# Early loads, idle transposes, split banks and weight sums made by need, in a kernel of linear attention and four experts

## The chip, the cores and the metric

One core of a Trainium2 chip. The metric is the device time of one execution in microseconds (us).

## The reference, cut to what matters

```python
# attention: batch 8, heads 8, sequence 576, head size 64
kv  = einsum('bhsd,bhse->bhde', k, v)
o   = einsum('bhsd,bhde->bhse', q, kv)
x   = o / sqrt(mean(o*o, -1) + 1e-6) * g_norm          # -> 4608 tokens x 512
# experts: E = 4, F = 1024
p   = probs / (probs.sum(-1) + 1e-9)
out = sum over e of  p[:, e] * (relu(x @ w1[e]) @ w2[e])
```

## The kernel before

The matrix products of the experts go by a scheme of the Strassen kind: seven products take the place of eight, at two levels in the first layer (49 small products for one step) and at one in the second. The price is sums: of weights, of tokens and of results. The work runs in 36 steps (4 experts x 9 chunks of 512 tokens). The attention of the eight batches is woven into the steps of the first expert, and each of the three later experts needs its sums of weights before its first step. The change of expert is called a switch below: steps 8 to 9, 17 to 18, 26 to 27.

A planner written in the kernel fixes the issue order of every engine while the kernel is built. Each operation has a key (about the step in which it is wanted) and a cost in us for each engine that may run it; the planner gives an operation to the first engine that is free in its model. Each engine then works through its list in order.

```python
def either(n):                       # a sum of n columns: VectorE or GpSimd
    return {"DVE": 0.17 + 0.00108 * n, "POOL": 0.1 + 0.0025 * n}

def combine(key, cost, out_, a, b, op, reads, writes):      # every sum of two SBUF tiles
    plan.add(key, cost, lambda eng: adder(eng).tensor_tensor(...), reads=reads, writes=writes)

BANKS = {"ub": 4, "db": 2, "ab": 2}   # PSUM banks: up-products, down-products, attention

def weights_1(e, key, step):          # first-layer weights of expert e: 4 loads, then
    ...
    form(key + 4 * step, 5, 21, 4, ALU.add)          # 4 sums of 128x1024
    ...
    for j, m in enumerate(OUTER):                    # and 7 x 4 sums of 128x256
        k2 = key + (8 + j) * step
        ...

attention(0, -2.0, 1.3, 0.1)
weights_1(0, -0.9, 0.02)
x_views = {0: x_forms(0, -0.2, 0.02)}                # sums of tokens: 4 + 7 x 4
...
            if e + 1 < E and c == NCH - 1:
                weights_1(e + 1, s + 0.0, 0.12)      # loads from s on, sums at s + 0.48 to s + 1.68
                weights_2(e + 1, s + 1.0, 0.12)
```

`POOL` is GpSimd, `DVE` is VectorE, `ACT` is ScalarE, `PE` is TensorE. The tiles lie in SBUF; PE writes its products into the eight PSUM banks of `BANKS`.

## Time and profile before

| | us |
|---|---|
| median of 6 runs | 1820.9 (1818.4 to 1821.4) |
| PE busy | 1784.6 of a span of 1818.3 |
| first expert product | 41.8 |
| first first-layer product of step 1 / 2 / 8 | 84.4 / 151.5 / 496.2 |
| last first-layer product (step 35) | 1790.8 |

### The profile page before, as it was taken

What the parts mean: (1) busy time and instruction counts of PE and PEld (TensorE: products, weight loads), DVE (VectorE), ACT (ScalarE), POOL (GpSimd) and SP (SyncE); (2) the same over time, 40 slices, a digit from 0 to 9 for tenths busy, and PEclk for the clock granted to TensorE, in tenths of its full rate; (3) what the DMA queues carried; (4) which work ended last, traced back from release to release, by engine and by line L of the source; (5) the groups of instructions that cost most, each with busy time, mean ns of one, the idle gap of its engine ahead of it and who ended that gap; (6) DMA issues with size and microseconds to landing.
All of it is one profiled execution on the core that took longest, in us unless ns stands there. A gap on an engine that the chain in (4) does not pass through costs nothing.

```text
span 1818.3 us, 32290 instructions
## 1 busy us (share of the span) xinstructions
PE 1784.6 (98%) x12496; PEld 1660.7 (91%) x12496; DVE 1126.2 (62%) x1841; ACT 608.4 (33%) x1345; POOL 475.1 (26%) x426
## 2 busy tenths in 40 slices
PE   5899999999999999999999999999999999999999
PEld 4889999999999999999999999999999999999997
DVE  6866665666676555555666555555566655556554
ACT  2544344443333333333333333333333333333331
POOL 4565554646364000000145000000036100000001
PEclk7999999999999999999999999999999999999999
DMA  9764444424433333334434333333434333343321
GB/s 231 179 167 141 128 139 126 135 95 139 132 109 119 117 114 115 114 113 134 136 130 152 118 118 118 118 118 121 147 127 163 117 115 117 118 118 116 115 74 35
DMA packets 192089, 228.96 MB, mean 126 GB/s; under 512 B 54464, under 2 KB 123328, under 8 KB 191936
## 3 DMA queue, kind: packets, MB, share of 16 engines
q1 hardware_dynamic: 191936, 226.89, 40.9%
q8 instruction: 99, 1.62, 0.4%
q14 instruction: 54, 0.44, 0.1%
HBM read 160.18 MB, written 66.65 MB: 125 GB/s over the span
## 4 chain that ended last, share of the span: by engine, by line
PE 94%; DVE 2%; SPq 2%; DMA 1%; issue 1%; POOL 0%; ACT 0%; DVEq 0%; ACTq 0%
PE ub L697 42%; PE db L831 29%; PE ab L831 18%; SPq L282 1%; PE ab L504 1%; PE ab L486 1%; DVE big L276 1%; PE ab L514 1%; PE ab L471 1%; DVE small L276 0%; DMA big<-in_moe_w_dram 0%; DMA small<-in_q_dram 0%; PE ab L553 0%; DVE big L718 0%; POOL big L276 0%
## 5 line engine op out<-in xcount | busy, mean ns | idle before, releaser
L831 PE MATMUL db<-big,big 128*128 128x256 f32 x2520 | 596.3, 380 | 1.7 <-DVE big L276 1.3
L697 PEld LDWEIGHTS ub<-small,big 128*128 128x128 f32 x3816 | 498.4, 192 | 23.4 <-issue 1.4
L697 PE MATMUL ub<-small,big 128*128 128x128 f32 x3816 | 513.5, 276 | 0.4 <-DVE big L718 0.4
L276 DVE TENSOR_TENSOR big<-big,big 128x1024 f32<-128x1024 f32 x343 | 474.8, 1384 | 55.1 <-ACT big L680 33.2
L831 PEld LDWEIGHTS db<-big,big 128*128 128x128 f32 x2520 | 455.2, 190 | 51.7 <-DVE big L276 1.5
L276 POOL TENSOR_TENSOR big<-big,big 128x1024 f32<-128x1024 f32 x85 | 209.0, 2462 | 1116.7 <-DVE big L276 976.1
L710 ACT ACTIVATE snap<-ub 128x256 f32<-128x256 f32 x756 | 285.5, 383 | 556.7 <-PE ub L697 500.8
L718 DVE TENSOR_TENSOR big<-ub,snap 128x256 f32<-128x256 f32 x756 | 307.0, 421 | 216.7 <-PE ub L697 163.1
L697 PE MATMUL ub<-small,w1y 128*128 128x128 f32 x2916 | 384.9, 276 | 2.2 <-DVE big L718 2.1
L697 PEld LDWEIGHTS ub<-small,w1y 128*128 128x128 f32 x2916 | 360.5, 192 | 7.9 <-DVE big L718 2.9
L831 PE MATMUL ab<-big,big 128*128 128x256 f32 x1512 | 357.4, 380 | 1.7 <-DVE small L788 1.7
L831 PEld LDWEIGHTS ab<-big,big 128*128 128x128 f32 x1512 | 273.2, 190 | 32.0 <-DVE small L788 2.1
L710 ACT ACTIVATE big<-ub 128x256 f32<-128x256 f32 x252 | 96.7, 384 | 414.6 <-PE ub L697 410.1
L788 DVE SCALAR_TENSOR_TENSOR small<-db,p_all,small 128x256 f32<-128x256 f32 x243 | 116.9, 481 | 139.8 <-PE db L831 139.2
L788 DVE SCALAR_TENSOR_TENSOR small<-ab,p_all,small 128x256 f32<-128x256 f32 x189 | 91.1, 482 | 177.3 <-PE ab L831 177.3
L680 ACT ACTIVATE big<-big 128x1024 f32<-128x1024 f32 x144 | 152.0, 1055 | 107.8 <-DVE big L276 104.8
L784 DVE TENSOR_SCALAR small<-db,p_all 128x256 f32<-128x256 f32 x72 | 34.6, 481 | 54.1 <-PE db L831 54.1
L425 POOL TENSOR_TENSOR rt<-ss,mhalf 128x8 f32<-128x8 f32 (+1 forms) x40 | 65.7, 1643 | 3.3
L421 POOL TENSOR_SCALAR ss<-ss 128x8 f32<-128x8 f32 (+1 forms) x40 | 15.6, 391 | 101.0 <-DVE ss L416 99.6
L416 DVE TENSOR_REDUCE ss<-small 128x8 f32<-128x512 f32 (+1 forms) x40 | 27.1, 678 | 22.3 <-ACT small L411 22.3
L504 PE MATMUL ab<-kvbd,small 128*128 128x128 f32 x256 | 38.3, 298 | 1.6 <-ACT kvbd L494 1.6
L432 DVE TENSOR_TENSOR small<-ab,rt 128x512 f32<-128x512 f32 (+1 forms) x40 | 27.4, 686 | 17.3 <-POOL rt L425 17.1
(63 smaller groups left out, 664.0 us busy)
## 6 DMA issues: line engine op xcount, KB each, us to landing
small<-x SPq DMA_DIRECT2D x189, 256.0 KB, 3.5
small<-x SPq DMA_DIRECT2D x189, 192.0 KB, 2.9
o<-small SPq DMA_DIRECT2D x108, 256.0 KB, 2.0
small<-o SPq DMA_DIRECT2D x108, 256.0 KB, 2.8
big<-in_moe_w_dram SPq DMA_DIRECT2D x32, 512.0 KB, 5.0
x<-small SPq DMA_DIRECT2D x63, 256.0 KB, 3.1
small<-in_q_dram SPq DMA_DIRECT2D x72, 128.0 KB, 3.9
kv<-in_k_dram SPq DMA_DIRECT2D x32, 288.0 KB, 3.5
```

Source lines behind the costliest of these rows:

```text
L276: lambda eng: adder(eng).tensor_tensor(out=out_(), in0=a(), in1=b(), op=op),
L416: lambda eng: nc.vector.reduce_sum(out=ss.ap[0:n, :], in_=rows(sq), axis=AX.X),
L425: nc.gpsimd.tensor_tensor(out=rt.ap[0:n, :], in0=ss.ap[0:n, :], in1=mhalf[0:n, :], op=ALU.pow)
L432: lambda eng: nc.vector.tensor_tensor(out=rows(x), in0=rows(raw), in1=rt.ap[0:n, :].unsqueeze(2).to_broadcast([n, H, D]), op=ALU.mult,),
L504: nc.tensor.matmul(raw.ap[:, rs], lhsT=qT.ap[:, rs], rhs=kb.ap[:])
L680: lambda eng: nc.scalar.activation(out=b.ap[:], in_=b.ap[:], func=ACT.Relu),
L697: nc.tensor.matmul(ps.ap[:, u * P:(u + 1) * P], lhsT=w1f[e][m][mm][1]()[:, u * P:(u + 1) * P], rhs=views[m][mm][1](), start=(mm in (1, 2, ...
L710: lambda eng: nc.scalar.activation(out=where(), in_=ps.ap[:, 0:HN], func=ACT.Copy),
L718: lambda eng: nc.vector.tensor_tensor(out=block(whole, a, t), in0=src.ap[:, 0:HN], in1=add_.ap[:], op=ALU.add),
L784: nc.vector.tensor_scalar_mul(out=acc[i].ap[:, cols], in0=ps.ap[:, 0:HN], scalar1=prob)
L788: nc.vector.scalar_tensor_tensor(out=acc[i].ap[:, cols], in0=ps.ap[:, 0:HN], scalar=prob, in1=acc[i].ap[:, cols], op0=ALU.mult, op1=ALU.add,)
L831: nc.tensor.matmul(ps.ap[:, 0:HN], lhsT=four(h[m])[:, kt // 2, t, kt % 2, :], rhs=w2f[e][m].ap[:, kt * HN:(kt + 1) * HN], start=(m in (1, ...
```

## The change

Its intent: load the first batch before the first weights, let its attention use all banks, make sums only when a product needs them, and keep PE's clock up with idle transposes until the experts have work for it.

```diff
-    BANKS = {"ub": 4, "db": 2, "ab": 2}
+    BANKS = {"u1": 2, "u2": 2, "db": 2, "ab": 2}
...
-        form(key + 4 * step, 5, 21, 4, ALU.add)
-        form(key + 5 * step, 6, 5, 1, ALU.subtract)
+        form(need + 0.25, 5, 21, 4, ALU.add)
+        form(need + 0.26, 6, 5, 1, ALU.subtract)
...
-                    k2, either(HN), parts[o][1], parts[a][1], parts[b][1], op,
+                    need + j / 7, either(HN), parts[o][1], parts[a][1], parts[b][1], op,
...
+            kind = "kv" if b or hp < 2 else "big"          # pairs 2 and 3 of batch 0 borrow big tiles
+            want = at(hp) - 0.25 if b else key - 1 + 0.1 * hp
...
+            combine(                                       # token sums: two 128-column sums in one
+                key + j / 7, either(2 * P), lambda t=t: two(t.ap[:, 0:2 * P]), ...
...
+                if eng == "PE" and busy[eng] <= t and 1.6 <= t and front < idle_until:
+                    ...                                    # a call of two identity transposes
...
-    weights_1(0, -0.9, 0.02)
-    x_views = {0: x_forms(0, -0.2, 0.02)}
+    weights_1(0, -2.5, 0.02, -0.35)
+    x_views = {0: x_forms(0, -0.3)}
...
-                weights_1(e + 1, s + 0.0, 0.12)
+                weights_1(e + 1, s + 0.0, 0.12, s + 0.6)
```

Cut: a group of products may not start before the group but one ahead of it has issued its last; spare tiles are kept back for loads alone; dependencies on the corner of a weight tile that is overwritten in place.

More of the change, by code (lines that the diff above doesn't have):

```diff
@@ L49, in __init__, with add @@
         self.ops = []
-    def add(self, key, cost, fn, reads=(), writes=(), parts=(), kb=0):
+    def add(self, key, cost, fn, reads=(), writes=(), parts=(), kb=0, after=()):
         op = Op(key, cost, fn, reads, list(writes) + list(parts), kb)
+        for o in after:
+            op.deps[o] = True
         for b in reads:
@@ L67, in add, with layout @@
         self.ops.append(op)
-    def layout(self, slots):
+        return op
+    def layout(self, slots, idle, idle_banks, idle_until):
         free = {k: [(0.0, i) for i in range(len(v))] for k, v in slots.items()}
@@ L80, in layout @@
         t = 0.0
-        wake = [0.0]
+        wake = [0.0, 1.6]
         left = len(self.ops)
@@ L96, in ready @@
             for k, n in need.items():
-                if len(free[k]) < n + (self.SPARE.get(k, 0) if op.key > front + 0.1 else 0):
+                if len(free[k]) < n + (self.SPARE.get(k, 0) if eng == "SP" and op.key > front + 0.1 else 0):
                     return None
@@ L150, in layout @@
                     break
+                if eng == "PE" and busy[eng] <= t and 1.6 <= t and front < idle_until:
+                    kind, spare = next((
+                        (k, f) for k in idle_banks for f in free[k] if f[0] <= t
+                    ), (None, None))
+                    if spare is not None:
+                        op = Op(front, {"PE": 0.23}, None, (), (), 0)
+                        op.start, op.eng, op.end = t, eng, t + 0.23
+                        op.fn = lambda eng, bank=slots[kind][spare[1]]: idle(bank)
+                        busy[eng] = op.end
+                        free[kind].remove(spare)
+                        free[kind].append((op.end, spare[1]))
+                        heapq.heappush(wake, op.end)
+                        order.append(op)
+                        moved = True
             if moved:
@@ L278, in combine, with load @@
         )
-    def load(key, buf, dst, src, kb, reads=()):
+    def load(key, buf, dst, src, kb, reads=(), also=()):
         plan.add(
             key, SPC, lambda eng: nc.sync.dma_start(out=dst(), in_=src), reads=reads,
-            parts=[buf], kb=kb,
+            parts=[buf] + list(also), kb=kb,
         )
@@ L330, in w2_src, with weights_1 @@
         return rows.rearrange("(kt p) d -> p kt d", p=P)
-    def weights_1(e, key, step):
+    def weights_1(e, key, step, need):
         f = {n: Buf("big", f"w1_{e}_{n}") for n in (1, 2, 21, 4, 5, 6, 7, 3)}
+        corner = {}
         for i, (n, dh, uh) in enumerate(((1, 0, 0), (2, 1, 0), (21, 0, 1), (4, 1, 1))):
+            corner[n] = Buf(None, f"w1c_{e}_{n}")
             load(
@@ L338, in weights_1 @@
                 lambda n=n: f[n].ap[:].rearrange("p (k u) -> p k u", k=2),
-                w1_src(e, dh, uh), 512,
+                w1_src(e, dh, uh), 512, also=[corner[n]],
             )
         def form(k_, o, a, b, op):
+            corner[o] = Buf(None, f"w1c_{e}_{o}")
             combine(
                 k_, either(1024), lambda: f[o].ap[:], lambda: f[a].ap[:], lambda: f[b].ap[:], op,
-                [f[a], f[b]], [f[o]],
+                [f[a], f[b], corner[a], corner[b]], [f[o], corner[o]],
             )
-        form(key + 4 * step, 5, 21, 4, ALU.add)
-        form(key + 5 * step, 6, 5, 1, ALU.subtract)
-        form(key + 6 * step, 7, 1, 21, ALU.subtract)
-        form(key + 7 * step, 3, 2, 6, ALU.subtract)
+        form(need + 0.25, 5, 21, 4, ALU.add)
+        form(need + 0.26, 6, 5, 1, ALU.subtract)
+        form(need + 0.5, 7, 1, 21, ALU.subtract)
+        form(need + 0.5, 3, 2, 6, ALU.subtract)
         w1f[e] = {}
         for j, m in enumerate(OUTER):
-            x, y = f[m], Buf("w1y", f"w1y_{e}_{m}")
+            x, low, y = f[m], corner[m], Buf("w1y", f"w1y_{e}_{m}")
             parts = {}
-            for n, at, (uq, kt) in ((1, 0, (0, 0)), (2, 1, (0, 1)), (7, 2, (1, 0)), (4, 3, (1, 1))):
-                parts[n] = (x, lambda x=x, uq=uq, kt=kt: two(x.ap[:])[:, kt, uq * HN:(uq + 1) * HN])
+            for n, (uq, kt) in ((1, (0, 0)), (2, (0, 1)), (7, (1, 0)), (4, (1, 1))):
+                parts[n] = (
+                    [x, low] if n == 7 else [x],
+                    lambda x=x, uq=uq, kt=kt: two(x.ap[:])[:, kt, uq * HN:(uq + 1) * HN],
+                )
             for n, at in ((5, 0), (6, 1), (3, 2)):
-                parts[n] = (y, lambda y=y, at=at: y.ap[:, at * HN:(at + 1) * HN])
-            k2 = key + (8 + j) * step
+                parts[n] = ([y], lambda y=y, at=at: y.ap[:, at * HN:(at + 1) * HN])
             for o, a, b, op in (
@@ L365, in weights_1 @@
                 combine(
-                    k2, either(HN), parts[o][1], parts[a][1], parts[b][1], op,
-                    [parts[a][0], parts[b][0]], [parts[o][0]],
+                    need + j / 7, either(HN), parts[o][1], parts[a][1], parts[b][1], op,
+                    parts[a][0] + parts[b][0], [low] if o == 7 else [y],
                 )
@@ L445, in attention @@
             n = f"{b}_{hp}"
-            kt, vt, qt = Buf("kv", f"k{n}"), Buf("kv", f"v{n}"), Buf("small", f"q{n}")
+            kind = "kv" if b or hp < 2 else "big"
+            kt, vt, qt = Buf(kind, f"k{n}"), Buf(kind, f"v{n}"), Buf("small", f"q{n}")
+            want = at(hp) - 0.25 if b else key - 1 + 0.1 * hp
             def kv_rows(t):
-                return t.ap[0:KP, :].rearrange("p (h j d) -> p h j d", h=2, d=D)
+                return t.ap[0:KP, 0:2 * KR * D].rearrange("p (h j d) -> p h j d", h=2, d=D)
             for r in range(2):
                 load(
-                    at(hp) - 0.25, qt,
+                    want, qt,
                     lambda qt=qt, r=r: qt.ap[:].rearrange(
@@ L459, in attention @@
                 load(
-                    at(hp) - 0.25, t,
-                    lambda t=t: t.ap[0:KP, :].rearrange("p (h x) -> p h x", h=2),
+                    want, t,
+                    lambda t=t: t.ap[0:KP, 0:2 * KR * D].rearrange("p (h x) -> p h x", h=2),
                     src[b, hs].rearrange("h (p j) d -> p h (j d)", j=KR), 288,
@@ L479, in attention @@
             )
-            bank = Buf("ab", f"kv{n}")
+            bank = Buf("ab" if b else "u1", f"kv{n}")
             kvbd[hp] = Buf("kvbd", f"kvbd{n}")
@@ L497, in attention @@
             plan.add(at(hp), {"ACT": 0.5}, diagonal, reads=[bank], writes=[kvbd[hp]])
-            raw = Buf("ab", f"raw{n}")
+            raw = Buf("ab" if b else "db", f"raw{n}")
             def attend(eng, raw=raw, qT=qT, kb=kvbd[hp]):
@@ L508, in attention @@
             scaled(at(hp + 0.4), n, raw, P, x)
-            bank = Buf("ab", f"xT{n}")
+            bank = Buf("ab" if b else "u2", f"xT{n}")
             def turn_x(eng, bank=bank, x=x):
@@ L587, with x_forms @@
     kept = {}
-    def x_forms(c, key, step):
+    def x_forms(c, key):
         xh = x_halves(c)
@@ L601, in x_forms @@
             combine(
-                key + j * step, either(NT), blocks[o][1], blocks[a][1], blocks[b][1], ALU.subtract,
+                key + (0.25, 0.26, 0.65, 0.8)[j], either(NT), blocks[o][1], blocks[a][1], blocks[b][1], ALU.subtract,
                 [blocks[a][0], blocks[b][0]], [blocks[o][0]],
@@ L611, in x_forms @@
                 parts[n] = (src, lambda ap=ap, kt=kt, th=th: ap()[:, kt, th * P:(th + 1) * P])
-            for n, at in ((5, 0), (6, 1), (7, 2), (4, 3)):
+            for n, at in ((5, 0), (7, 1), (6, 2), (4, 3)):
                 parts[n] = (t, lambda t=t, at=at: t.ap[:, at * P:(at + 1) * P])
-            for o, a, b in ((5, 12, 1), (6, 3, 5), (7, 3, 12), (4, 2, 6)):
+            combine(
+                key + j / 7, either(2 * P), lambda t=t: two(t.ap[:, 0:2 * P]),
+                lambda ap=ap: ap()[:, :, P:2 * P], lambda ap=ap: two(ap()[:, 0, :]),
+                ALU.subtract, [src], [t],
+            )
+            for o, a, b in ((6, 3, 5), (4, 2, 6)):
                 combine(
-                    key + (4 + j) * step, either(P), parts[o][1], parts[a][1], parts[b][1],
-                    ALU.subtract, [parts[a][0], parts[b][0]], [parts[o][0]],
+                    key + j / 7, either(P), parts[o][1], parts[a][1], parts[b][1],
+                    ALU.subtract, [parts[a][0], parts[b][0]], [t],
                 )
@@ L626, in x_forms @@
             plan.add(
-                key + 0.5, {"SP": 0.16}, store_raw, reads=[src], parts=[kept[c, m]], kb=192,
+                key + 0.9, {"SP": 0.16}, store_raw, reads=[src], parts=[kept[c, m]], kb=192,
             )
             plan.add(
-                key + 0.5, SPC,
+                key + 0.9, SPC,
                 lambda eng, t=t, keep=keep: nc.sync.dma_start(out=keep[:, 3 * P:], in_=t.ap[:]),
@@ L651, in x_again @@
                 for n, b, at in (
-                    (1, r, 0), (2, r, 1), (3, r, 2), (5, t, 0), (6, t, 1), (7, t, 2), (4, t, 3)
+                    (1, r, 0), (2, r, 1), (3, r, 2), (5, t, 0), (7, t, 1), (6, t, 2), (4, t, 3)
                 )
@@ L658 @@
     hidden = {}
+    last = []
     def four(b):
@@ L686, in up @@
             whole = made[m] = Buf("big", f"m{n}")
-            bank = {1: Buf("ub", f"u1_{n}"), 2: Buf("ub", f"u2_{n}")}
+            bank = {1: Buf("u1", f"u1_{n}"), 2: Buf("u2", f"u2_{n}")}
             snap = {}
@@ L691, in up @@
                 if mm == 5:
-                    bank[2] = Buf("ub", f"u3_{n}")
+                    bank[2] = Buf("u2", f"u3_{n}")
                 ps = bank[1 if mm in (1, 6, 7, 4) else 2]
@@ L701, in product @@
                         )
-                plan.add(
-                    key, pe(2, P), product, reads=[w1f[e][m][mm][0], views[m][mm][0]], writes=[ps]
-                )
+                op = plan.add(
+                    key, pe(2, P), product, reads=w1f[e][m][mm][0] + [views[m][mm][0]], writes=[ps],
+                    after=last[-2:-1] if mm in (1, 2) else (),
+                )
+                if mm == 3:
+                    last.append(op)
                 def copy(to, where, ps=ps, key=key):
@@ L853 @@
     attention(0, -2.0, 1.3, 0.1)
-    weights_1(0, -0.9, 0.02)
-    x_views = {0: x_forms(0, -0.2, 0.02)}
+    weights_1(0, -2.5, 0.02, -0.35)
+    x_views = {0: x_forms(0, -0.3)}
     weights_2(0, 0.0, 0.02)
-    norm_probs(0.1)
+    norm_probs(0.3)
     for e in range(E):
@@ L867 @@
                 if e == 0 and c + 1 < NCH:
-                    x_views[s + 1] = x_forms(c + 1, s + 0.75, 0.03)
+                    x_views[s + 1] = x_forms(c + 1, s + 0.7)
                 else:
@@ L872, with idle @@
             down(s, e, c)
-    order = plan.layout(slots)
+    def idle(bank):
+        for r in range(2):
+            nc.tensor.transpose(bank[:, r * P:(r + 1) * P], ident[:], ident[:])
+    order = plan.layout(slots, idle, ("u1", "u2", "db"), 0.0)
     with tc.manual_schedule(engines={ENG.PE, ENG.DVE, ENG.Activation, ENG.Pool, ENG.SP}):
```

## The prediction

> **What bounds the kernel now.** I read the busy table of the page first, then its 40 slices, then the busy time of each engine in stretches of 10 us, then the matmul, VectorE, GpSimd and DMA-queue timelines of the first 100 us, and last the start-to-start distance of every matmul record.
>
> ```profile
> PE 1784.6 (98%) x12496; PEld 1660.7 (91%) x12496; DVE 1126.2 (62%) x1841; ACT 608.4 (33%) x1345; POOL 475.1 (26%) x426
> PE   5899999999999999999999999999999999999999
> PEclk7999999999999999999999999999999999999999
> ```
>
> TensorE (PE) bounds the kernel, and only the first slices show idle time or a low clock. So a change at the start is worth what it takes out of the first 100 us and little else.
>
> ```profile
> 20.00:30.00 10.00, 8.21 (x72) 7.09 (x72) 9.47 (x13) 2.93 (x8) 5.12 (x3) 0.58 1.18 246
> 30.00:40.00 10.00, 1.48 (x6) 0.79 (x6) 8.99 (x19) 1.28 (x2) 7.92 (x9) 0.50 0.80 207
> 40.00:50.00 10.00, 9.98 (x63) 9.37 (x64) 9.33 (x17) 4.72 (x11) 9.84 (x17) 0.72 1.10 236
> 50.00:60.00 10.00, 6.88 (x70) 6.31 (x70) 9.90 (x15) 3.13 (x10) 6.50 (x5) 0.96 0.82 268
> ```
>
> Columns after the length are the busy us of PE, weight load, DVE, ACT and POOL, then the clock. Between 30 and 40 us PE does 1.48 us of work while DVE (VectorE) is 90% busy: DVE makes weight sums while the first batch's attention waits for it. The PE timeline shows the wait and the first expert product (L697):
>
> ```profile
> 28.28 2.08 PE L504 MATMUL ab<-kvbd,small 128*128 128x128 f32 x8 [0.55 <-ACT kvbd L494]
> 34.70 1.11 PE L514 MATMUL ab<-ident,small 128*128 128x128 f32 x4 [4.33 <-DVE small L432]
> 40.02 1.09 PE L514 MATMUL ab<-ident,small 128*128 128x128 f32 x4 [4.21 <-DVE small L432]
> 41.76 1.91 PE L697 MATMUL ub<-big,big 128*128 128x128 f32 x8
> 57.85 0.71 PE L697 MATMUL ub<-big,w1y 128*128 128x128 f32 x4 [2.74 <-DVE big L718]
> 84.41 0.71 PE L697 MATMUL ub<-small,w1y 128*128 128x128 f32 x4 [2.10 <-DVE big L718]
> ```
>
> For every matmul I took the distance to the next start and subtracted the median of its kind (0.112 us for an L697 record, 0.216 for L831). These excesses sum to 47.7 us: 24.8 us before 41.76 us, 22.9 us after it. Of the 22.9, 12.4 lie between 41.7 and 110 us: 3.2 at a low clock, the gaps at 52, 55, 82 and 96 us (6.4), and small change. After 110 us there are 9.9 us, of which 3.5 are three gaps at changes of expert (501, 950, 1366 us). Add the 5.8 us before the first matmul and the start costs 30.6 us. The 1759.9 us of medians are work that the change does not remove: the ceiling of any gain is about 50 us.
>
> **What the Trainium skill says.** *TensorE: Matmul & The Clock Gate*, "Part 1: The HAM clock gate": the array runs at half rate by default and gets the full rate after about one 3.4 us window of sustained work. The trace agrees: the same eight L504 records take 2.08 us at 28 us and 1.06 at 66 us; the records grant full clock only from 18.2 to 21.6 us, then half until 45.5 us, and half again from 59.2 to 62.6 us, after the pause at 55 us.
>
> *DMA: Bandwidth & Descriptors*, "Queues, rings and completion order": each engine consumes a queue's descriptors in ring order. Here all loads are on one queue[...]. The trace agrees: first-expert weights land from 14.7 to 19.0 us, and the keys and values of head pair 2, issued after them, at 20.95 us, of pair 3 at 23.55 us.
>
> *SBUF — State Buffer*, "SBUF: two separate sides": GpSimd and a DVE operation with two SBUF inputs take a shared port pair exclusively, and the loser blocks for the whole instruction. The trace agrees, and this limits how fast the sums can be made: here a DVE operation that takes 0.28 us when free takes 2.45 us behind a GpSimd one.
>
> ```profile
> 75.50 2.67 POOL L276 TENSOR_TENSOR big<-big,big 128x1024 f32<-128x1024 f32 x1 [4.38 <-DVE big L718]
> 75.87 2.45 DVE L276 TENSOR_TENSOR small<-big,small 128x128 f32<-128x128 f32 x1
> ```
>
> **The change, part by part.**
>
> *Loads.* All four pairs now come ahead of the weights (pairs 2 and 3 borrow large tiles). Pairs 0 and 1 land as before, at 7.56 and 11.08 us. From the packets, a back-to-back pair costs 2 x 0.7 us for q and 2 x 1.23 for k and v: 3.86 us. So pair 3 lands at 11.08 + 7.7 = 18.8 us (before: 23.55), and four weight tiles at 1.45 us each at 20.2 to 24.6 us (before: 14.7 to 19.0). The second-layer weights end near 36 us, as before.
>
> *Attention.* Matmuls followed v by about 1 us before (7.56 to 8.52). At full clock pair 3 is then: key-value product 19.8 to 20.65, a transpose and three idle calls to 21.75, attend (0.9) to 22.65. From attend to the transpose of x the trace of pair 0 shows 4.2 us (square, reduce, power, scale, one after the other); the issue order instead puts 24 idle calls and one transpose there, 24 x 0.22 + 0.44 = 5.7 us, so the idle work, not the chain, sets the time: 28.35, plus 0.44, gives the **first expert product at 28.8 us instead of 41.76: 13.0 us earlier**. DVE no longer stands in between: in its new order only six small sums (1.8 us) lie between pair 3's reduction and its scaling.
>
> *Idle transposes.* 59 calls of two transposes stand before the first product, 16 after it, because the filler runs until the next batch's attention has begun. They should have the clock at full rate by about 8 us and keep it: gain 3.2 us of low-clock excess after the first product; the gain inside the attention is in the 28.8. Cost: 16 x 0.22 = 3.5 us if nothing else waits there; I count 2, as some fall into waits.
>
> *Sums by need.* The same first-expert weight sums, but now during the first products. The token sums of a chunk go from 28 small operations in the inner level to 21; VectorE tensor-tensor operations fall from 1285 to 1247, GpSimd's from 380 to 317. Is supply fast enough? By issue order, up to the sums for the last product group, POOL has 31 us of work after its last power, of which some 25 hold the ports, and DVE has some 16 us of two-SBUF-input operations. Wholly serial that is 41 us; the trace shows pairs overlapping partly (a GpSimd 256-column operation with a VectorE one between: 0.86 us, against 0.69 + 0.335), so I take 80%: 33 us from about 26.5, done at 59.5 us. PE wants them 31.7 us after its first product, at 60.5. So supply just keeps up on the whole, and I allow 4 us of local waits. The normalisation of probabilities (3.4 us in one DVE operation, behind the gap at 55 us) moves later.
>
> *Banks.* The four up-product banks are split into two pairs, and a group may not start before the last product of the group but one. In the steady part only about 1 us per expert is lost now, so nothing much can be won; the second bank of a group is freed by a DVE sum about 1 us after its last product, and the next group needs it three products (1.3 us) and mostly one L831 block (1.73 us) later. I count nothing.
>
> *Sum.* First product earlier: -13.0; one transpose of batch 1 that used to precede it: +0.4. Excess after the first product, before 22.9; after: 4 of waits for sums, 2 of idle calls, 3 for the second batch's sums (as the gaps at 82 and 96 us), 8.5 for all later (9.9 before, fewer operations): 17.5, so -5.4. Together -18.0 from 1821.2: **1803 us**.
>
> **The rivals.** (1) *The sums become the wait.* The weights land 5.6 us later than now while their first use comes 13 us sooner, and DVE is over 90% busy from 20 to 60 us already. If the ports serialise fully, 41 us end at 67.5 instead of 60.5 and 7 us are added to the 4: 1810. Against it: DVE was idle 10 us between 60 and 100 us and POOL 22 us, slack that an earlier start can use. (2) *The idle calls cost more than they give.* Their number is fixed in the issue order; where data comes sooner than assumed they hold PE up, 0.22 us each. With all 16 lost and the 24 in front of the last transpose run partly cold, 4 us more: 1807. (3) *Everything behind gets better too.* If the waits at 55 to 96 us and half of the later excess vanish, excess falls to about 9: 1795. (4) *The new bank pools stall the steady part.* There are 252 groups; 0.1 us in each would be 25 us and would eat the gain: 1828. The distances above speak against it, but it is the one way to a slower kernel.
>
> **Range and chances.** Rivals 1 to 3 span 1795 to 1810; I widen a little: 1793 to 1812. Faster by over 2% means below 1784.8, which needs 36 of the ceiling's 50 us; the landing of pair 3 at 18.8 us alone makes that nearly impossible: 2%. Slower by over 2% needs rival 4 at twice that size: 1%. Within 2%: 97%.
>
> **What would show it.** The first L697 record near 29 us (over 33: the load or idle step is wrong); full clock from about 8 us on and no second dip (else the idle step is wrong); no wait over 1 us on L432 before the first product; PE waits on L276 and L718 between 29 and 70 us summing to about 4 us (over 8: rival 1); excess per group after 600 us near zero as now (else rival 4). A first product on time with a total above 1812 would make the prediction wrong through the supply of sums or the banks; a total below 1793 through the later excess.

## More of the kernel before

The prediction shows the main lines. Two more are of use later, from the timelines of GpSimd and VectorE in the first 30 us (start, length, engine, line, operation, result<-operands, shapes, count):

```profile
20.36 4.84 POOL L276 TENSOR_TENSOR big<-big,big 128x1024 f32<-128x1024 f32 x2
21.04 1.95 DVE L276 TENSOR_TENSOR w1y<-big 128x256 f32<-128x256 f32 x1
22.91 3.37 DVE L276 TENSOR_TENSOR big<-big,big 128x1024 f32<-128x1024 f32 x1
```

A VectorE sum of 256 columns, 0.42 us elsewhere, takes 1.95 us here, and one of 1024 columns, else 1.22, takes 3.37. "Busy" on VectorE therefore also counts time in which an operation stands still.

## The result, and the profile after

Ratios are the mean time of one kernel's runs over that of the other's of the same rounds, so not quite the ratio of the medians that I quote.

The changed kernel takes **1838.7 us** (median of 6; 1832.1 to 1840.1) against 1820.9: ratio 1.0092 (95% interval 1.0076 to 1.0109). It is slower, by 17.7 us in the medians, and the prediction of 1803 us with a range of 1793 to 1812 is wrong. That is under 2%, so the class that the prediction gave 97%, "within 2%", did come; but the interval is clear of 1, and the sign was wrong.

The page's busy line, slices and clock, and the busy time in the stretches that the prediction showed of before:

```profile
PE 1804.1 (98%) x12646; PEld 1680.9 (91%) x12646; DVE 1146.6 (62%) x1816; ACT 606.0 (33%) x1345; POOL 479.2 (26%) x388
PE   9799999999989999999989999999989999999999
PEclk9999999999999999999999999999999999999999
...
20.00:30.00 10.00, 10.00 (x109) 9.76 (x108) 6.72 (x13) 3.48 (x7) 6.83 (x7) 1.00 0.95 244
30.00:40.00 10.00, 8.15 (x68) 7.17 (x66) 9.38 (x12) 4.76 (x10) 9.03 (x9) 1.00 1.02 263
40.00:50.00 10.00, 7.14 (x48) 6.74 (x47) 8.47 (x9) 1.57 (x5) 9.83 (x9) 0.83 1.04 226
50.00:60.00 10.00, 5.91 (x38) 5.13 (x37) 9.21 (x10) 2.62 (x8) 9.92 (x11) 0.83 0.50 166
```

The first slice is full now, as intended, in part with idle calls. But the second slice is a 7 now, and three later slices, where the switches are, show an 8 that was a 9 before. And look at the counts of DVE (VectorE): 9.2 us busy with only 10 operations between 50 and 60 us, where before it made 15 in 9.9.

The PE timeline, where before it had its waits and its first expert product (L728 is the old L697):

```profile
26.26 3.66 PE L910 MATMUL u<-ident 128*128 128x128 f32 x32
29.75 0.60 PE L539 MATMUL u<-ident,small 128*128 128x128 f32 x4
30.19 1.06 PE L728 MATMUL u<-big,big 128*128 128x128 f32 x8
...
48.77 0.71 PE L728 MATMUL u<-small,big 128*128 128x128 f32 x4 [2.50 <-DVE big L294]
...
54.45 0.91 PE L728 MATMUL u<-small,w1y 128*128 128x128 f32 x4 [4.09 <-DVE big L752]
```

The first product comes at 30.2 us instead of 41.8, and the wait before the last transpose is gone, filled by idle calls. Then PE stands still for VectorE.

Where the 11.6 us went is best seen by the time of the first first-layer product of each step, read from the matmul records of both traces ("lag", below, is the last column, for any kernel):

| first first-layer product of step | before | after | after minus before |
|---|---|---|---|
| 0 | 41.8 | 30.2 | -11.6 |
| 1 | 84.4 | 85.1 | +0.7 |
| 2 | 151.5 | 153.7 | +2.3 |
| 8 | 496.2 | 497.5 | +1.3 |
| 10 (after the first switch) | 589.9 | 597.1 | +7.2 |
| 17 | 912.3 | 919.5 | +7.2 |
| 19 (after the second) | 1006.1 | 1019.1 | +13.0 |
| 26 | 1328.6 | 1341.5 | +13.0 |
| 28 (after the third) | 1422.4 | 1442.4 | +20.0 |
| last first-layer product (step 35) | 1790.8 | 1810.7 | +20.0 |

So there are two losses: 13.9 us in steps 0 and 1, which eat the gain, and 5.9, 5.8 and 7.0 us at the three switches. The steps between are as fast as before. (These are single profiles; at e5 you see that steps 0 and 1 can differ by 5 us from one profile to the next.)

**What a stall is made of.** The timelines of VectorE and GpSimd in the changed kernel, between the two waits of PE at 46 and 50 us:

```profile
44.73 8.38 DVE L294 TENSOR_TENSOR big<-big 128x256 f32<-128x256 f32 x2
53.03 0.94 DVE L294 TENSOR_TENSOR small<-big 128x256 f32<-128x256 f32 x1
53.89 0.41 DVE L752 TENSOR_TENSOR big<-u,snap 128x256 f32<-128x256 f32 x1
...
45.42 0.72 POOL L294 TENSOR_TENSOR w1y<-big 128x256 f32<-128x256 f32 x1
46.10 2.33 POOL L294 TENSOR_TENSOR big<-big,big 128x1024 f32<-128x1024 f32 x1
48.40 0.90 POOL L294 TENSOR_TENSOR w1y<-w1y,big 128x256 f32<-128x256 f32 x1
49.26 2.33 POOL L294 TENSOR_TENSOR big<-big,big 128x1024 f32<-128x1024 f32 x1
51.57 1.25 POOL L294 TENSOR_TENSOR small<-big,big 128x512 f32<-128x512 f32 x1
```

Two VectorE sums of 256 columns take 8.38 us (the single records 3.99 and 4.47), though each is 0.42 us of work. GpSimd works back to back all the while. Behind the two stands L752, the sum that empties a product's bank, at 53.89 us, and PE resumes at 54.45 us, when it is done. L752 itself, one of whose operands is in PSUM, is as quick as ever (0.41 us); but VectorE works through its list in order, so it is late as well.

The same at a switch. The VectorE sum shown, one before it (1.95 us) and two after it (0.94 and 0.83) are of a size that takes 0.42 us elsewhere, and PE waits for the L752 behind them:

```profile
943.74 4.84 POOL L294 TENSOR_TENSOR big<-big,big 128x1024 f32<-128x1024 f32 x2 [4.28 <-issue]
946.41 2.46 DVE L294 TENSOR_TENSOR big<-big 128x256 f32<-128x256 f32 x1
950.52 0.74 DVE L752 TENSOR_TENSOR big<-u,snap 128x256 f32<-128x256 f32 x2
950.98 0.71 PE L728 MATMUL u<-small,big 128*128 128x128 f32 x4 [2.98 <-DVE big L752]
```

PE's waits around this switch (920 to 980 us; total us, times, longest), first of the changed kernel, then of the one before:

```profile
PE u L728 <- DVE big L752: 3.0, 1, 3.0
PE db L865 <- DVE small L822: 1.7, 1, 1.7
```

```profile
PE ab L831 <- DVE small L788: 0.9, 1, 0.9
```

Theory P: GpSimd's sums block VectorE's, and what PE waits for stands behind them; making the weight sums by need has drawn them together (by their keys, from s + 0.48 to s + 1.68 into s + 0.6 to s + 1.46), and PE has no slack there. Rivals: L, there are simply too many sums for the time; B, the split banks and the order of the groups stall PE; I, the idle calls hold PE up.

### The profile page after: what moved, and what is told of

The parts are those of the page before. It is cut to its first block, busy times and chain, and to the rows that moved or that the text cites. A ratio compares the mean times of both kernels' runs of the same rounds, so it can differ in the third digit from the quotient of the medians. Undisturbed runs are those within 1.5% of the kernel's fastest.

```text
span 1838.3 us, 32455 instructions
## 1 busy us (share of the span) xinstructions
PE 1804.1 (98%) x12646; PEld 1680.9 (91%) x12646; DVE 1146.6 (62%) x1816; ACT 606.0 (33%) x1345; POOL 479.2 (26%) x388
## 4 chain that ended last, share of the span: by engine, by line
PE 94%; DVE 4%; issue 1%; POOL 0%; DMA 0%; ACT 0%; SPq 0%; DVEq 0%; POOLq 0%
PE u L728 42%; PE db L865 29%; PE ab L865 18%; DVE big L294 1%; PE ab L529 1%; PE ab L511 1%; DVE w1y L294 1%; DVE small L294 1%; PE ab L496 1%; PE ab L539 1%; DVE big L752 0%; PE u L910 0%; PE ab L578 0%; POOL rt L448 0%; DVE small L822 0%
## 5 line engine op out<-in xcount | busy, mean ns | idle before, releaser
L728 PEld LDWEIGHTS u<-small,big 128*128 128x128 f32 x3816 | 498.8, 192 | 32.4 <-DVE big L752 6.7
L728 PE MATMUL u<-small,big 128*128 128x128 f32 x3816 | 515.5, 277 | 10.3 <-DVE big L752 6.2
L294 DVE TENSOR_TENSOR big<-big,big 128x1024 f32<-128x1024 f32 x342 | 468.7, 1372 | 59.6 <-ACT big L711 38.8
L294 POOL TENSOR_TENSOR big<-big,big 128x1024 f32<-128x1024 f32 x86 | 210.2, 2450 | 1124.6 <-DVE big L294 991.9
L744 ACT ACTIVATE snap<-u 128x256 f32<-128x256 f32 x756 | 284.7, 382 | 519.8 <-PE u L728 443.4
L752 DVE TENSOR_TENSOR big<-u,snap 128x256 f32<-128x256 f32 x756 | 309.2, 421 | 222.9 <-PE u L728 162.7
L728 PE MATMUL u<-small,w1y 128*128 128x128 f32 x2916 | 389.2, 277 | 8.9 <-DVE big L752 8.7
L728 PEld LDWEIGHTS u<-small,w1y 128*128 128x128 f32 x2916 | 364.7, 193 | 16.5 <-DVE big L752 5.0
L865 PEld LDWEIGHTS ab<-big,big 128*128 128x128 f32 x1512 | 275.9, 192 | 30.2 <-ACT big L711 0.4
L744 ACT ACTIVATE big<-u 128x256 f32<-128x256 f32 x252 | 96.5, 383 | 460.0 <-PE u L728 458.8
L818 DVE TENSOR_SCALAR small<-db,p_all 128x256 f32<-128x256 f32 x72 | 34.5, 480 | 45.1 <-PE db L865 41.9
L444 POOL TENSOR_SCALAR ss<-ss 128x8 f32<-128x8 f32 (+1 forms) x40 | 14.2, 355 | 93.7 <-DVE ss L439 92.3
L294 POOL TENSOR_TENSOR small<-small 128x256 f32<-128x256 f32 x32 | 28.3, 886 | 30.2 <-PE u L728 18.1
L294 POOL TENSOR_TENSOR small<-big,small 128x128 f32<-128x128 f32 (+1 forms) x35 | 24.6, 703 | 40.1 <-DVE small L294 25.8
```

What stands on the lines that cost most here:

```text
L294: lambda eng: adder(eng).tensor_tensor(out=out_(), in0=a(), in1=b(), op=op),
L728: nc.tensor.matmul(ps.ap[:, u * P:(u + 1) * P], lhsT=w1f[e][m][mm][1]()[:, u * P:(u + 1) * P], rhs=views[m][mm][1](), start=(mm in (1, 2, ...
L744: lambda eng: nc.scalar.activation(out=where(), in_=ps.ap[:, 0:HN], func=ACT.Copy),
L752: lambda eng: nc.vector.tensor_tensor(out=block(whole, a, t), in0=src.ap[:, 0:HN], in1=add_.ap[:], op=ALU.add),
L818: nc.vector.tensor_scalar_mul(out=acc[i].ap[:, cols], in0=ps.ap[:, 0:HN], scalar1=prob)
L865: nc.tensor.matmul(ps.ap[:, 0:HN], lhsT=four(h[m])[:, kt // 2, t, kt % 2, :], rhs=w2f[e][m].ap[:, kt * HN:(kt + 1) * HN], start=(m in (1, ...
```

## The experiments

Each is the changed kernel with the edit shown, unless it says before.

### The switches: keys, banks, idle calls, GpSimd

**e1_w1keys**, the sums of experts 1 to 3 at their old keys:

```diff
-        form(need + 0.25, 5, 21, 4, ALU.add)
+        form(key + 4 * step if early else need + 0.25, 5, 21, 4, ALU.add)     # early = e > 0; so for all sums
```

> The changed kernel, with the first-layer weight sums of experts 1 to 3 back at their old keys (spread from the start of the step before the switch); those of expert 0 stay by need. Compared with before, the changed kernel loses 5.4, 5.7 and 6.8 us at the three expert switches (up-step 8 to 10, 17 to 18 and 26 to 27). Theory A (the sums by need bunch on VectorE and GpSimd just before and after the switch): each switch loses under 2 us, total about 1822 us. Rival B (the split banks and the group order stall there): no change, about 1838 us.

Measured 1820.9 us (ratio 1.0003, 0.9988 to 1.0019). The lag behind the kernel before goes from +3.3 us at step 8 to +4.9 at the end, where the changed kernel's goes from +1.3 to +20.0. Theory A of the expectation holds: the sums by need cost some 17 us at the switches.

**e2_banks**, one pool of four banks and no order of groups:

```diff
-    BANKS = {"u1": 2, "u2": 2, "db": 2, "ab": 2}
+    BANKS = {"ub": 4, "db": 2, "ab": 2}
-                    after=last[-2:-1] if mm in (1, 2) else (),
+                    after=(),
```

> The changed kernel with the up-product banks back in one pool of four and no order between groups; sums by need stay. Theory A: the switches still lose 5 to 7 us each, total 1835 to 1840. Rival B: the switches lose under 2 us, total about 1822.

Measured 1836.6 us (1.0086, 1.0068 to 1.0104); the switches still lose 15.6 us together. B falls.

**e3_noidle**, no idle transposes:

```diff
-    order = plan.layout(slots, idle, ("u1", "u2", "db"), 0.0)
+    order = plan.layout(slots, idle, ("u1", "u2", "db"), -1e9)
```

> The changed kernel without the idle transposes. If step 0 is bound by the supply of sums and not by PE, the first expert product moves 0 to 4 us and the end of step 0 (85.1 us) by at most 2 us: total 1836 to 1841. If the 16 idle calls after the first product hold PE up, it gets faster by up to 3.5 us; if the clock they keep up matters, slower by 3 us or more.

Measured 1837.1 us (1.0091, 1.0076 to 1.0106). The first product comes even sooner, at 28.4 us, with the clock at half from 27.5 to 30.9, from 48.0 to 54.8 and from 82.1 to 92.3 us (20.4 us in all; 10.2 us up to 90 us in the changed kernel); step 1 begins at 87.2 us instead of 85.1, and at the end nothing is left of the difference. Neither the clock nor the held-up PE is worth anything that these runs resolve. I falls.

**e5_nopool**, no GpSimd sum from step 8 on:

```diff
     def combine(key, cost, out_, a, b, op, reads, writes):
+        if key >= 7.9:
+            cost = {"DVE": cost["DVE"]}
```

> The changed kernel with every sum from step 8 on given to VectorE alone (GpSimd makes none). Theory P (VectorE operations with two SBUF inputs stand blocked behind GpSimd sums, and the sums that PE waits for stand behind them in VectorE's queue): the switch losses vanish, each under 2 us, total 1818 to 1824, although VectorE has more to do. Rival L (VectorE has simply too much to do there): the switches lose more than now, total over 1842.

Measured 1817.7 us (0.9988, 0.9971 to 1.0004): 21 us faster than the changed kernel, by giving VectorE *more* work. The lag goes from -1.6 us at step 8 to -2.5 at the end, with the sums still by need. PE has no wait at all around the second switch, and the second and third lose nothing (they gain 1.7 us each). The first still loses 3.8 us up to step 10, more than the 2 us expected. GpSimd sums with keys under 7.9 are still running there. One, from 500.84 us and 2.36 long, stands beside the first of these lines, and PE's wait is behind it:

```profile
500.95 2.52 DVE L297 TENSOR_TENSOR small<-small 128x256 f32<-128x256 f32 x1
504.79 0.71 PE L731 MATMUL u<-x_rem,w1y 128*128 128x128 f32 x4 [1.52 <-DVE big L755]
```

Another such wait, of 1.17 us, ends at 496.39 us. So at the switches it is not the order of the sums by itself and not their amount (L), but the order together with GpSimd (P). The clock shows it too: in the profiled run of the changed kernel it drops to half for 3.4 to 6.8 us at each switch, after the waits; here it doesn't. One reserve holds for all runs without GpSimd sums: the planner lays out VectorE's list anew in each, so the edit changes more than the blocking. What ties the gain to the blocking is the time of single sums, shown at e13.

One more thing to learn from this run: up to 457 us the order of operations on PE, VectorE, ScalarE and GpSimd is the same in the changed kernel, e1, e5 and e11, and yet their step 1 began at 85.1, 86.5, 81.5 and 84.5 us. Without GpSimd sums, e10 and e13 below, of the same order up to 570 us, have 80.6 and 81.0. So with GpSimd sums one profile of steps 0 and 1 differs from the next by up to 5 us with nothing changed up to there, and must not be read more finely than that.

**b1_nopool**, the kernel before with the same edit:

> The kernel before with no GpSimd sums from step 8 on. It loses about 1.3 us at each of three switches; if GpSimd's blocking is behind that too, the total falls by 2 to 5 us, to about 1817; if VectorE then has too much to do, it rises.

Measured 1821.6 us (1.0007, 0.9992 to 1.0022). A miss: no gain. Its lag is +1.0 us at step 8, +5.6 after the first switch, +3.9 and +2.2 after the others. It gains 1.7 us at each of two switches and loses 4.6 at the first. The trace shows why: the last GpSimd sums with keys under 7.9 (498.02 us, two in 4.91 us) hold small token sums on VectorE (2.13 and 2.43 us, from 498.38 and 500.64), and PE waits 1.65 and 2.07 us behind them, up to 504.06 and 506.84 us. It is the edge of the edit, not too much work for VectorE.

**e11_both**, e1 and e5 together:

> The changed kernel with both cures at the switches: old keys of the first-layer sums for experts 1 to 3 and no GpSimd sums from step 8. If they cure the same waits, the total is that of the better one, 1816 to 1819; if each removes a part of its own, 1812 to 1815.

Measured 1819.6 us (0.9991, 0.9976 to 1.0006), between e5 and e1: nothing is added. The two cure the same waits.

### Steps 0 and 1: where the 11.6 us went

**e6_w2late**, the second-layer sums of expert 0 later, so that the two long GpSimd sums of 46 and 49 us are not there:

```diff
-        form(key + 4 * step, 5, 12, 1, ALU.subtract)
+        form(key + late + 4 * step, 5, 12, 1, ALU.subtract)      # late = 0.6 for expert 0; so for all four
```

> The changed kernel with the four second-layer weight sums of expert 0 keyed 0.6 of a step later. In the changed kernel two of them ran on GpSimd at 46.1 and 49.3 us, 2.33 us each, while VectorE sums stood blocked for up to 4 us each and PE waited 2.5 and 4.1 us. Theory P (blocking by GpSimd sums): step 0 ends 3 to 6 us earlier (about 80 instead of 85.1), total about 1834. Rival L (the whole supply of sums, not these blocks): the same work comes later in the same step, end of step 0 within 2 us, total about 1838.

Measured 1835.8 us (1.0082, 1.0064 to 1.0100), step 1 at 84.5 us. Not told from the changed kernel. The two waits fell from 2.5 and 4.1 us to 0.2 and 2.5, but one of 5.0 us came at the turn of the step (80.88 us). By the chain of its trace it lies behind ScalarE, which waits for two GpSimd sums of results (73.73 us, 3.19, and 77.00, 2.41). That is a second way in which GpSimd costs time: not by blocking, but as the slower of the two (2.4 us against 1.2 for a sum of 1024 columns). The runs without GpSimd sums take away both ways, and no run parts them.

**e8_bigdve**, the 128x1024 sums of steps 0 and 1 kept off GpSimd:

```diff
+        if key < 2 and cost["POOL"] > 2:
+            cost = {"DVE": cost["DVE"]}
```

> The changed kernel with the 128x1024 sums of steps 0 and 1 kept off GpSimd (VectorE does each in about 1.2 us; GpSimd takes 2.4 and blocks VectorE meanwhile). Theory P: step 0 ends 3 us earlier or more, total 1830 to 1836. Rival L (VectorE has too much to do): step 0 ends later than 85.1, total over 1840.

Measured 1838.9 us (1.0097, 1.0082 to 1.0113), step 1 at 84.8 us. A miss for P as I had put it: the long sums alone are not the cause; GpSimd's many short ones do it too. At 52.04 us a VectorE sum of 1024 columns takes 4.23 us beside short GpSimd sums back to back, most of 0.7 us.

**e7_actcopy**, the first-layer sums of expert 0 become copies on ScalarE:

```diff
-            combine(                        # in weights_1
+            (moved if e == 0 else combine)( # moved: nc.scalar.activation(out, in_=a, func=Copy)
```

> Wrong result on purpose: the first-layer weight sums of expert 0 become copies of one operand on ScalarE, so that VectorE and GpSimd are rid of 4 large and 28 small operations. If the supply of sums binds step 0 in the changed kernel, step 0 now ends 7 to 12 us earlier (73 to 78 instead of 85.1) and most of the 11.6 us that the first expert product gained are kept; total 1827 to 1832. If something else binds (banks, loads, ScalarE), it ends within 3 us of 85.

Measured 1834.6 us (1.0070, 1.0054 to 1.0087), result wrong. PE now has hardly a wait from 30 to 70 us (the gaps beyond the usual ones add up to some 3 us, against some 15 in the changed kernel). So it is the sums that starve PE in step 0, no bank and no load. Then one wait remains, in the PE, GpSimd and VectorE timelines:

```profile
77.11 1.22 PE L736 MATMUL u<-small,w1y 128*128 128x128 f32 x4 [4.60 <-DVE big L760]
...
69.20 5.16 POOL L294 TENSOR_TENSOR big<-big,big 128x1024 f32<-128x1024 f32 x2 [0.74 <-ACT big L553]
...
68.99 3.18 DVE L294 TENSOR_TENSOR small<-big 128x256 f32<-128x256 f32 x2
72.09 2.43 DVE L294 TENSOR_TENSOR small<-big,small 128x128 f32<-128x128 f32 x1
76.63 0.42 DVE L760 TENSOR_TENSOR big<-u,snap 128x256 f32<-128x256 f32 x1
```

It is the stall of above again, at the turn of the step: two GpSimd sums of results hold up three small token sums for 5.5 us. This is why step 1 began only 5.4 us earlier (79.7 us), where I expected 7 to 12. The switches lose 21.1 us, so the total, above the 1827 to 1832 expected, is not told from the changed kernel's.

**e9_nopool01**, no GpSimd sum in steps 0 and 1:

```diff
+        if key < 2:
+            cost = {"DVE": cost["DVE"]}
```

> The changed kernel with no GpSimd sums in steps 0 and 1; GpSimd sums stay from key 2 on, so the switch losses stay (some 18 us). Theory P (a GpSimd sum blocks VectorE, so that GpSimd's help in step 0 is worth little): step 0 ends between 78 and 86 us although VectorE alone makes all sums, total 1832 to 1839. Rival L (the sums are simply too much work and GpSimd's part counts): step 0 ends 8 to 12 us later than 85.1, total about 1848.

Measured 1823.3 us (1.0020, 1.0004 to 1.0037): 15 us faster than the changed kernel, better than P had said. Step 1 begins at 79.9 us, step 2 at 140.4 instead of 153.7, step 8 is 12.2 us *ahead* of the kernel before: the whole gain of the early first product is there. VectorE alone makes the sums sooner than VectorE and GpSimd together. The switches then lose 15.4 us.

**e10_nopoolall**, no GpSimd sum anywhere (`if True:` in the place of the condition):

> The changed kernel with no GpSimd sum anywhere. Theory P: the switches lose nothing, as in the run without GpSimd sums from step 8 (1817.7), and steps 0 to 8 end within 4 us of that run: total 1814 to 1822. Rival L: VectorE has too much to do while the batches of expert 0 are in attention: total over 1828.

Measured 1803.8 us (0.9908, 0.9893 to 0.9922), far below the 1814 to 1822 that P had said: the steps up to 8, too, went faster than in e5 (step 8 begins at 484.9 us against 494.6), and the gain at the switches came on top. But the result was wrong (relative error 0.041). An assertion put into the code that builds the kernel found why: in this issue order a merge of step 9 stands before the load of the stored sums that it adds to. Both kernels leave this order unstated, and it happened to be right in theirs.

**e13_fixed**, the same with the order stated:

```diff
             plan.add(key - 0.4, {"DVE": 0.5}, fn, reads=[ps, probs], parts=[acc[i]])
+            if e:
+                plan.ops[-1].deps[got[i]] = True       # got[i]: the load of acc[i]
```

> The run without any GpSimd sum gave a wrong result: in its issue order a merge of step 9 stood before the load of the stored sums that it adds to, an order that neither kernel states. Here the merges depend on that load; else the same. Expected: correct, 1802 to 1806 us, so that the time was not owed to the mistake. If the missing order made it fast, over 1808.

Measured **1803.9 us** (0.9912, 0.9897 to 0.9927), correct: 16 us faster than before and 35 us faster than the changed kernel. VectorE's groups of sums between 26 and 90 us (line, engine, operation, names, shapes, count | busy us, mean ns | idle before), first the changed kernel, then this one:

```profile
L294 DVE TENSOR_TENSOR big<-big,big 128x1024 f32<-128x1024 f32 x12 | 17.3, 1445 | 0.4 <-ACT big L711 0.4
L294 DVE TENSOR_TENSOR big<-big 128x256 f32<-128x256 f32 x6 | 11.2, 1885 | 0.0
L294 DVE TENSOR_TENSOR small<-big,small 128x128 f32<-128x128 f32 x7 | 7.7, 1093 | 0.0
```

```profile
L297 DVE TENSOR_TENSOR big<-big,big 128x1024 f32<-128x1024 f32 x16 | 19.3, 1214 | 0.0
L297 DVE TENSOR_TENSOR big<-big 128x256 f32<-128x256 f32 x7 | 2.9, 414 | 0.0
L297 DVE TENSOR_TENSOR small<-big,small 128x128 f32<-128x128 f32 x10 | 2.8, 280 | 0.0
```

The same operations take 414 ns instead of 1885, and 280 instead of 1093. Three groups that had 36.2 us for 25 sums have 25.0 us for 33. The list of PE's waits between 30 and 90 us shrinks from 12.6 us (8.1 for L752, 4.1 for L294, 0.4 others) to 0.3 us.

### What the change is worth without GpSimd's sums

**b2_nopoolall**, the kernel before with e13's two edits:

> The kernel before without any GpSimd sum, with the same added order. If the gain of the last run is GpSimd's alone and the change gives nothing, this is as fast, 1801 to 1806. If the change's earlier first product (11.6 us) counts once GpSimd is out of the way, this stays 8 to 14 us slower than the last run, 1811 to 1818.

Measured 1808.0 us (0.9933, 0.9918 to 0.9948). Neither of the two expectations: 12.1 us come from taking GpSimd out, and the change adds 4.1 us, not 8 to 14 (a small difference: the slowest run of e13 and the fastest of this kernel are 1805.7 and 1805.8). Its first product is 9.8 us later than e13's (40.0 against 30.2), and step 2 begins 6.0 us later.

**e14_noidle**, e13 without idle transposes (edit as in e3):

> As e13_fixed without the idle transposes. With PE no longer starved of sums, the clock they keep up should now count: low clock for some 4 to 10 us after the first product, 1 to 5 us slower than e13_fixed. If they are worth nothing here either, within 1 us.

Measured 1803.7 us (0.9908, 0.9892 to 0.9925): no difference, though the clock was at half for 13.6 us, from 27.7 to 31.1 and from 41.4 to 51.6 us. PE's waits between 30 and 90 us in this run say why:

```profile
PE ab L596 <- DVE small L458: 5.7, 1, 5.7
PE ab L499 <- DMA small<-in_q_dram: 2.2, 1, 2.2
```

In e13 32 idle calls stand where PE has its largest wait here (37.95 to 45.1 us). So "PE 100% busy" on e13's page is partly idle work, and PE has slack in step 0 even without GpSimd: a faster PE is worth nothing that these runs resolve. What that wait is for is not VectorE's amount of work. L458 is VectorE's scaling of attention, and VectorE itself stood idle 1.8 us before it, for GpSimd: a GpSimd operation on 8 columns (L447) took 2.91 us, 0.2 at its quickest, beside three VectorE sums back to back (39.87 to 42.55 us), and GpSimd's power another 1.63. So the blocking goes the other way too, and e13 still has some 7 us in step 0 in which PE does idle work.

**e15_keys**, e13 with all first-layer sums at their old keys:

> As e13_fixed with the first-layer sums of all experts at their old keys, none by need. If making them by need is what lets PE start without a wait, step 0 ends 4 us or more later than with it (80.6) and the total rises to 1807 to 1813; if without GpSimd the order of the sums is of no account, within 2 us of e13_fixed.

Measured 1803.5 us (0.9907, 0.9892 to 0.9922): no difference. Without GpSimd's sums it is of no account which of the two orders the weight sums have.

**e12_sums0**, this same edit for all experts in e5 (GpSimd sums up to step 7):

> As the last, and the first-layer sums of expert 0 also at their old early keys: only loads, banks, idle transposes and token sums of the change are left in step 0. If the order of sums in step 0 matters, step 0 ends more than 3 us away from the 81.5 to 85.1 us of the by-need runs; if only their amount matters, within 3 us, and the total is within 3 us of the last run's.

Measured 1818.5 us (0.9989, 0.9971 to 1.0007), within 3 us of e11, with step 1 at 87.3 us against 84.5: no effect of the order in step 0 is told from the 5 us by which such profiles differ.

**b3_loads**, b2 with the load order of the change alone:

```diff
+            want = at(hp) - 0.25 if b else key - 1 + 0.1 * hp      # and big tiles for pairs 2 and 3
-    weights_1(0, -0.9, 0.02)
+    weights_1(0, -0.9, 0.02, 1.6)                                 # loads 1.6 earlier, sums as before
```

> The kernel before without any GpSimd sum (b2_nopoolall, 1808.0 us), with one part of the change added: all first-batch loads ahead of the first-layer weights. If the earlier loads are what the change is still worth once GpSimd is out of the way, this reaches 1803 to 1805.5 us. If it is the banks, the sums by need or the merged token sums, it stays at 1807 to 1809.

Measured 1807.8 us (0.9928, 0.9912 to 0.9945): nothing. The first product moves only to 37.4 us. What gives the 4.1 us, banks for the attention, merged token sums or the way they work together with the loads, stays open; putting the banks back in e13 could not be tried, since the planner finds no order for it (the build stops with "no operation can start" at 99.6 us of its model).

## Why the prediction was wrong, point by point

- **"First expert product at 28.8 us instead of 41.76: 13.0 us earlier."** Right in mechanism, off by 1.4 us: 30.19. The 1.4 us were lost before that: pair 3's key-value product began at 21.18, not 19.8 (its values landed at 20.45, not 18.8). The idle calls set this time, as foreseen: 24 of them and a transpose stand between attend and the last transpose. Without them (e3) it is 28.4.
- **"Full clock from about 8 us on and no second dip."** Half right. The full clock came at 10.4 us, when PE had run transposes alone (its first product of keys and values starts at 10.71), and held to 41.1; then it dropped, after the waits. The term of 3.2 us for the clock was wrong in its sense, not only in size: with PE waiting for sums, the clock is worth nothing that e3 and e14 resolve.
- **"I take 80%: 33 us ... So supply just keeps up on the whole, and I allow 4 us of local waits."** This is the step that failed first. The excess from the first product to 110 us, measured as in the prediction, is about 25 us where the sum had 9 (4 + 2 + 3), with the idle calls not even counted in. I had taken 0.86 us for a pair of short sums as the rule of how the two engines overlap. In the trace VectorE does not take turns: it loses the port to several GpSimd sums one after the other (8.38 us for two sums), and L752 waits behind. e7 and e9 show that the sums, and GpSimd among them, are what binds. My rival 1 named the cause, and its sign came (PE's waits for L294 and L752 between 29 and 70 us sum to 8.6 us, over the 8 that I had set); but I sized it at 7 us over the 4 and no more; moreover I wrote that GpSimd had been idle 22 us between 60 and 100 us, which is its busy time; idle were 18.
- **"8.5 for all later (9.9 before, fewer operations)."** This failed worst. The switches cost 18.7 us more than before. The diff has the key `s + 0.6` for experts 1 to 3, and the prediction said nothing of it: it counted the sums by need of the first expert alone. e1 shows that this one line is worth 17 us, and e5 that it is so through GpSimd.
- **"Banks ... I count nothing."** Right: e2 is within noise of the changed kernel. But rival 4, the banks, was called "the one way to a slower kernel", and that was wrong: the kernel is slower, and not by the banks. Nor by the idle calls of rival 2 (e3).
- **Readings that were off.** "The normalisation of probabilities (3.4 us in one DVE operation ...)" was taken for a cost. It was a stall, there to be seen: the addition to 36 columns that takes 3.38 us in the kernel before takes 0.18 in the changed one and in e13. Of tensor-tensor operations the profile counts 1260 on VectorE and 342 on GpSimd, not 1247 and 317. And 12.4 and 9.9 us, the two parts of the excess, make 22.3, not 22.9. The last two move the sum by little.
- **The ceiling of about 50 us** was sound: the best version, e13, takes out 16.

In sum: predicted -18.0; measured +17.7. Of the difference of some 36 us, about 19 is the switches, 16 the missing supply in steps 0 and 1, and 1 the first product.

## What to carry to other kernels

Before moving work to an idle GpSimd, look whether VectorE's operations beside it grow longer: here the mean of one group of 128x256 sums was 1.89 us beside GpSimd and 0.41 without it, and giving *all* sums to VectorE made the kernel faster (1803.9 against 1838.7 us) though it had more to do. An engine's busy share does not show this; the mean time of one operation with and without the neighbour does. And when a diff makes something "by need", go through every place that uses that line: the slack that the early version had may be what hid another engine's stalls.

## What the Trainium skill lacked or had wrong

- *SBUF — State Buffer*, "SBUF: two separate sides" says that the loser blocks while the winner's instruction lasts. It does not say that a waiting VectorE operation can lose again to the next GpSimd one: two sums of 0.42 us stood 3.99 and 4.47 us while GpSimd ran six sums back to back (45.4 to 53.7 us).
- No page follows such a block into the schedule: the sum that empties a bank (L752), with an operand in PSUM, stayed at 0.42 us itself but came late behind blocked sums, and PE with it (waits of 2.5 to 4.6 us).
- No page says how far such a kernel's profiles differ with nothing changed: four with the same order on all engines had step 1 begin at 81.5 to 86.5 us; two without GpSimd sums, at 80.6 and 81.0.
